# Where ScalarE's held passes stand between the projection groups of a gated mix of attention and gMLP

## The chip, the cores and the metric

The kernel runs on 1 core of a Trainium2 chip. The metric is the time of one execution on the device in microseconds (us). Each kernel has a profile of one execution; times inside it count from the start of its span.

## What is computed

One input x of 2048 tokens by 1024 goes through two branches, which a gate mixes per token:

```python
g = sigmoid((x * gate_w).sum(-1))
# A: 32 heads of 32; each token attends to itself and 7 earlier tokens, 2 apart
q, k, v = split(x @ wqkv)                  # 1024 x 3072
a = softmax(q . k[t - 2w], w = 0..7) @ v[t - 2w] @ wo
# B: gMLP, 3584 columns in two halves of 1792
z = gelu(x @ w_in); z1, z2 = z[:, :1792], layernorm(z[:, 1792:])
b = (z1 * (w_sp @ z2 + b_sp)) @ w_out      # w_sp is 2048 x 2048
out = g * a + (1 - g) * b
```

## The kernel before

TensorE computes all products; ScalarE evicts most of them from PSUM (copy or gelu); VectorE does the attention itself as elementwise products and folds; SP issues the transfers. q, k and v go through scratch in HBM and come back in another layout.

**Heads** are taken in 8 groups of 4. `qkv_tile(g, j)` (L931 on) projects one sixteenth of the tokens on a group's q, k and v: 8 matmuls of 384 columns (L936), a cast by ScalarE (L939) and, every fourth tile, three stores (L944).

**z2** has 4 column blocks of 448. The blocks 0 and 1 are plain tiles (L370, gelu L379). The blocks 2 and 3 are computed by `z2_group(u)`, u = 0 to 7, each for 256 tokens: a scheme of seven products of 4 matmuls of 449 columns (L451) in place of eight. The 449th column carries the gate's sum. Between the products stand four qkv tiles (of the groups 3 and 4 of heads), so that TensorE has work while ScalarE moves partial results. In order:

1. product a11 into bank pa; ScalarE copies pa to a second bank (the seed, L467); tile 1;
2. products s1 into bank pd and s2 onto pa; ScalarE keeps both (L445); tile 2;
3. the two late gelus of the group before (`z2_late`: L379 and a one-column L457 each); products a12 onto the seed and s3 onto pa; gelu of the seed; a third keep (L445); tile 3;
4. products s4 onto pd and a22 onto pa; two sums by VectorE (L483, and L484, which reads pd); gelu of pa; tile 4.

The product s2 writes a bank that the seed copy L467 reads, and a22 one that the third keep reads, so TensorE waits for ScalarE's queue at these two places. A tile or product that takes over pd's bank waits for L484.

**Attention** runs on VectorE beside all this, one group of heads after the other: the products q.k (L505) and their folds (L509, L512), the maximum and the difference (`soft_a`, L526 to L529), the exponentials on ScalarE (L550), sums and reciprocal (`soft_b`, L554 to L560), the products with v (L570) and their folds (L576, L577, L573). ScalarE needs another table of functions for the exponentials than for gelu; each change is a table load in its queue.

**The order of the work** is set when the program is written out, by a planner in the kernel. `Beat` counts the time of the matmuls written so far. `beat.at(t, fn)` writes a piece of work out when that clock passes t. The steps of attention carry a time at which VectorE should be free; a step is written out once that is no more than `lead` ahead of the clock: 3.0 us in general (`LEAD`), 1.0 in the groups (`GROUP_LEAD`). Engines run their queues strictly in this order.

In the groups three kinds of passes of ScalarE are **held back**. `hold_back` puts the exponentials (`exp_now`) and the absolute sum over an attention output (`o_norm_now`, L679) into the list `held`, and `release()` (L539) empties it. It is called three times in a group: behind the cast of tile 3, behind the gelu of pa, and behind the cast of tile 4. The third kind are the squares (L1011), sums of squares of one z2 tile of 1792 columns for the layer norm. Eight are owed over the groups (`prep["owed"]`: one each for u = 1 to 6, two for u = 7). They are written at the end of a group if nothing held was released in it, all that are owed at once (`squares_owed`).

**Behind the groups** come the groups 5 to 7 of heads with the rest of the z2 blocks 0 and 1, which use six banks of one pool and two of another in turn. ScalarE takes on the absolute sums over rows of w_sp (L758) there. Then come z1 (L1084, gelu L1087) and the mixing groups (L1101), seven products each again, with ScalarE's seed copies (L1125), keeps (L1111, L1113) and VectorE's sums (L1117); the column sums L799 on VectorE must be done before them.

Of the kernel before, what the change touches and what calls it, by code (L numbers as in the profile page):

```python
# [35 lines left out]
DN = ZC + 2  # L36
BEAT = 1.0 / 2360.0
LEAD = 3.0
GROUP_LEAD = 1.0
MIX_LEAD = 0.5  # L40
NU = S // 256
FL = FH // 2
# [20 lines left out]
def kernel(  # L63
# [276 lines left out]
    beat = Beat()  # L340
# [37 lines left out]
    def z2_out(src, i, c, scale):  # L378
        nc.scalar.activation(z2[:, i, ZC * c:ZC * (c + 1)], src, ACT.Gelu_apprx_tanh, scale=scale,  # L379
                             accum_out=s1[:, 4 * i + c:4 * i + c + 1])  # L380
# [61 lines left out]
    def z2_keep(ps):  # L442
        out = z2_snaps[z2_kept[0] % 5]
        z2_kept[0] += 1
        nc.scalar.copy(out, ps[:, 0:DN - 1])  # L445
        return out

    def z2_product(ps, w, v, first):
        for k in range(4):
            lhsT = w[:, k // 2, k % 2, :] if len(w.shape) == 4 else w[:, k, :]  # L450
            nc.tensor.matmul(ps[:, 0:DN - 1], lhsT, v[:, k, 0:DN - 1], start=(first and k == 0), stop=(k == 3),  # L451
                             skip_group_check=True)
        beat.run(4 * (DN - 1))

    def z2_late(i, src, scale):
        z2_out(src[:, 0:ZC], i, 3, scale)
        nc.scalar.activation(gl_s[:, i:i + 1], src[:, ZC:ZC + 1], ACT.Copy, scale=scale)  # L457
# [3 lines left out]
    def z2_group(u, tiles):  # L461
        v = tokens[u]
        scale = zinv
        pa, pd = [psum.tile([P, 512], F32, name="ps", tag="ps") for _ in range(2)]
        z2_product(pa, v.a11, m11, True)
        pb = seeded.tile([P, 512], F32, name="seed", tag="sd")
        nc.scalar.copy(pb[:, 0:DN - 1], pa[:, 0:DN - 1])  # L467
        tiles.pop(0)()
        z2_product(pd, v.s1, r1, True)
        p5 = z2_keep(pd)  # L470
        z2_product(pa, v.s2, r2, False)
        u2 = z2_keep(pa)
        tiles.pop(0)()
        while z2_wait:
            z2_late(*z2_wait.pop(0))
        z2_product(pb, v.a12, m21, False)
        z2_out(pb[:, 0:ZC], 2 * u, 2, scale)
        z2_product(pa, v.s3, r3, False)
        u3 = z2_keep(pa)
        tiles.pop(0)()  # L480
        some = release()
        z2_product(pd, v.s4, m22, False)
        TT(p5, p5, u3, ALU.add)  # L483
        TT(u2, u2, pd[:, 0:DN - 1], ALU.add)  # L484
        beat.on_vector(1.3)
        z2_product(pa, v.a22, r4, False)
        z2_out(pa[:, 0:ZC], 2 * u + 1, 2, scale)
        some = release() or some
        tiles.pop(0)()
        some = release() or some  # L490
        prep["owed"] += min(u, 1) + u // 7
        if not some:
            squares_owed(u)
        z2_wait.extend([(2 * u + 1, p5, scale), (2 * u, u2, scale)])

    L = att_L
# [34 lines left out]
    held, exp_wait = [], []  # L531
# [4 lines left out]
        else:  # L536
            fn()

    def release():  # L539
        some = bool(held)  # L540
        while held:
            held.pop(0)()
        return some

    def exp_now():
        if exp_wait:
# [185 lines left out]
    prep = {"at": 1e12, "normed": 0, "done": False, "attended": False, "heads": 0, "mixing": False, "groups": False, "owed": 0}  # L732
# [21 lines left out]
    def load_nat(a, slot):  # L754
        sync.dma_start(slot, wsp_v[a])

    def row_norm(a, slot):
        nc.scalar.activation(slot, slot, ACT.Abs, accum_out=l1[:, a:a + 1])  # L758
# [46 lines left out]
    def stats(i):  # L805
        sl = slice(i - 7, i + 1)
        s1v = s1[:, 4 * (i - 7):4 * (i + 1)].rearrange("p (i c) -> p i c", c=4)
        nc.vector.tensor_reduce(mean[:, sl], s1v, AX.X, ALU.add)
        nc.vector.tensor_scalar(mean[:, sl], mean[:, sl], 1.0 / FH, None, ALU.mult)
        nc.vector.tensor_tensor(var[:, sl], mean[:, sl], mean[:, sl], ALU.mult)  # L810
        nc.vector.scalar_tensor_tensor(var[:, sl], s2[:, sl], 1.0 / FH, var[:, sl], ALU.mult, ALU.subtract)
        nc.vector.tensor_scalar(var[:, sl], var[:, sl], 0.0, EPS, ALU.max, ALU.add)
        nc.gpsimd.tensor_tensor(rstd[:, sl], var[:, sl], cm05[:], ALU.pow)
        beat.on_vector(0.8)

    def norm(ii):
        nc.vector.tensor_scalar(z2h[:, ii, :], z2[:, ii, :], mean[:, ii:ii + 1], rstd[:, ii:ii + 1],
                                ALU.subtract, ALU.mult)
        beat.on_vector(0.75)
        prep["normed"] += 1  # L820
# [110 lines left out]
    def qkv_tile(g, j, plain=True):  # L931
        wgt = wg_slots[g % 3]
        ps = bank() if plain else psum.tile([P, 512], F32, name="ps", tag="ps")
        for kt in range(KT):
            lhsT = xT[:, kt, j * P:(j + 1) * P] if g == 0 else _sub_ap(xh_flat, kt * S + j, [[NJ, P]])
            nc.tensor.matmul(ps[:, 0:3 * C].rearrange("p (t c) -> p t c", t=3), lhsT, wgt[:, :, kt, :],  # L936
                             start=(kt == 0), stop=(kt == KT - 1))
        st = (stage_early if g < 5 else stage_slots)[stg[0] % 3]
        nc.scalar.copy(st[:, j % 4, :].rearrange("p (t d h) -> p t d h", t=3, h=HG),  # L939
                       ps[:, 0:3 * C].rearrange("p (t h d) -> p t d h", t=3, h=HG))  # L940
        if j % 4 == 3:
            row, step, first = (C, P * C, (j - 3) * P) if g == 0 else (NJ * C, C, j - 3)
            for n, (t_d, off) in enumerate(((q_d, g * S), (k_d, g * (S + 16) + 16), (v_d, g * (S + 16) + 16))):
                sync.dma_start(bass.AP(tensor=t_d.tensor, offset=t_d.offset + (off + first) * C,  # L944
                                       ap=[[row, P], [step, 4], [1, C]]), st[:, :, n * C:(n + 1) * C])
            stg[0] += 1
        projected[g] += 1
        beat.run(KT * 3 * C)
# [46 lines left out]

    square = [0]

    def squares_owed(u):
        while prep["owed"] > 0:
            prep["owed"] -= 1  # L1000
            squares(u)

    def squares(u=NU):
        i = square[0]
        square[0] += 1
        out_, src = junk[:, 0:FH], z2[:, i, :]
        if u < 4:
            out_ = wg_slots[2].rearrange("p t k c -> p (t k c)")[:, 0:FH]
        elif i < 8:
            out_, src = z2[:, 12:16, 0:ZC], src.rearrange("p (a f) -> p a f", a=4)  # L1010
        nc.scalar.activation(out_, src, ACT.Square, accum_out=s2[:, i:i + 1])  # L1011
        if i % 8 == 7:
            beat.at(beat.now + 4.0, lambda i=i: stats(i))
            for ii in range(i - 7, i + 1):
                beat.at(beat.now + 10.0, lambda ii=ii: norm(ii))
# [8 lines left out]
    tiles = [lambda g=g, j=j: qkv_tile(g, j, False) for g in (3, 4) for j in range(NJ)]  # L1024
    beat.lead = GROUP_LEAD
    prep["groups"] = True
    for u in range(NU):
        if u == 4:
            load_wg(5)
        z2_group(u, tiles)  # L1030
# [1 line left out]
        z2_late(*z2_wait.pop(0))  # L1032
    beat.lead = LEAD
    prep["groups"] = False
    release()
    squares_owed(NU)
    t = beat.now
    for n in range(16):
        beat.at(t + (0.5 + 2.5 * n if n < 3 else 5.2 * n), lambda n=n: load_nat(n, nat_slots[n % 3]))
        beat.at(t + 11.5 + 5.2 * n, lambda n=n: row_norm(n, nat_slots[n % 3]))  # L1040
    for g in range(5, NG):
# [4 lines left out]
        for j in range(NJ):  # L1046
            qkv_tile(g, j)
            n = NJ * (g - 5) + j
            if n % 3 == 2:
                n = n // 3  # L1050
# [3 lines left out]
    t = beat.now  # L1054
# [4 lines left out]
    t = beat.now  # L1059
# [133 lines left out]
    for n in range(2 * NU):  # L1193
        u, fb = n // 2, n % 2
        t = beat.now
# [21 lines left out]
    t = beat.now  # L1217
# [183 lines left out]
```

## Time and profile before

| | |
|---|---|
| time, median of 3 runs | 676.68 us (675.35 to 677.0) |
| profiled execution | 676.31 us |
| its span | 674.5 us |
| granted clock of TensorE | 1.0 |
| busy: TensorE, VectorE, ScalarE, GpSimd | 663.6, 575.7, 442.4, 12.0 us |

| stretch, us | what | TensorE busy | VectorE busy | ScalarE busy | DMA share |
|---|---|---|---|---|---|
| 92.5 to 184.2 | projection groups | 85.94 of 91.7 | 85.97 | 69.09 | 0.38 |
| 184.2 to 270 | heads 5 to 7, rest of z2 | 85.80 of 85.8 | 83.39 | 76.57 | 0.89 |
| 270 to 368 | z1 | 98.00 of 98 | 96.21 | 74.80 | 0.78 |
| 368 to 533 | mixing | 164.82 of 165 | 150.57 | 116.82 | 0.73 |

How to read it: the span is the part of an execution that the profiler records. In lists of waits a line gives engine and line, what it waited for, the total, the number of times and the longest. In a timeline a line gives start, duration, engine, line, operation and, in brackets, the idle time ahead of it and what ended it. "PE" is TensorE, "DVE" VectorE, "ACT" ScalarE. Matmuls overlap: the next starts before the one ahead has ended, so starts tell more than ends. In a table of stretches each engine has its busy time and its number of instructions, then come the granted clock, the DMA share and GB/s.

### The profile page before, as it was taken

To read this page: it belongs to the slowest core of one execution; us is meant where nothing else is said; L and a number is where in the kernel's file an instruction comes from. 1 tells how busy PE (TensorE), PEld (TensorE's weight loads), DVE (VectorE), ACT (ScalarE), POOL (GpSimd) and SP (SyncE) were. 2 spreads that over 40 slices of the span, in tenths; PEclk is the share of its full clock that TensorE was granted. 3 is DMA by queue.
4 is the path that set the end of the run, shared out by engine and by line. 5 is a ranking of instruction groups with operands and counts; after the bars stand their busy time and mean duration, and the time that the engine had idled before them with its cause. 6 is when DMAs were issued, how large, how long until landed. Compare 5 with 4: busy or idle time off the path is not lost.

```text
span 674.5 us, 9601 instructions
## 1 busy us (share of the span) xinstructions
PE 663.6 (98%) x3564; PEld 390.0 (58%) x3564; DVE 575.7 (85%) x660; ACT 442.4 (66%) x774; POOL 12.0 (2%) x68
## 2 busy tenths in 40 slices
PE   9999999989999999999999999999999999999998
PEld 4568876656677777555555555555555544444443
DVE  4567999998899999999999999999988787954745
ACT  4437676778879899898764568686767764522122
POOL 0000000000020000001000000000000000000000
PEclk9999999999999999999999999999999999999999
DMA  8999574244188999995966686549679599486211
GB/s 233 176 245 263 107 202 131 89 102 112 48 224 217 283 274 290 253 318 162 289 219 204 163 208 178 135 138 219 157 188 295 138 235 265 88 169 144 60 62 63
DMA packets 229919, 123.92 MB, mean 184 GB/s; under 512 B 191088, under 2 KB 217456, under 8 KB 229872
## 3 DMA queue, kind: packets, MB, share of 16 engines
q1 hardware_dynamic: 229872, 123.31, 69.2%
q8 instruction: 28, 0.46, 0.3%
q14 instruction: 19, 0.16, 0.1%
HBM read 63.97 MB, written 37.82 MB: 151 GB/s over the span
## 4 chain that ended last, share of the span: by engine, by line
PE 88%; DVE 7%; ACT 2%; DMA 1%; issue 1%; SPq 0%; ACTq 0%
PE ps L1101 37%; PE ps L936 15%; PE ps L1084 11%; PE seed L1101 7%; PE ps L370 6%; PE sd L936 5%; PE sd L1084 4%; PE ps L451 2%; DVE arena L509 1%; DVE arena L505 1%; DVE arena L570 1%; PE sd L370 1%; DMA arena<-in_B_w_in_dram 1%; DMA q_d<-arena 1%; DVE arena L437 0%
## 5 line engine op out<-in xcount | busy, mean ns | idle before, releaser
L1101 PE MATMUL ps<-arena 128*128 128x448 f16 (+1 forms) x1296 | 263.5, 363 | 0.2 <-ACT seed L1125 0.2
L1101 PEld LDWEIGHTS <-arena 128*128 128x128 f16 x1519 | 148.5, 98 | 154.3 <-issue 0.7
L936 PEld LDWEIGHTS <-arena 128*128 128x128 f16 (+1 forms) x1024 | 141.5, 138 | 31.2 <-issue 1.7
L936 PE MATMUL ps<-arena 128*128 128x384 bf16 x800 | 142.5, 326 | 1.3 <-DVE arena L484 1.3
L1084 PEld LDWEIGHTS <-arena 128*128 128x128 f16 x512 | 50.0, 98 | 46.6
L509 DVE TENSOR_TENSOR arena<-arena 128x4096 bf16<-128x4096 bf16 (+1 forms) x64 | 74.0, 1157 | 1.7
L1084 PE MATMUL ps<-arena 128*128 128x448 bf16 x384 | 75.4, 352 | 0.0
L505 DVE TENSOR_TENSOR arena<-arena 128x8192 bf16<-128x8192 bf16 x16 | 70.8, 4422 | 4.9 <-DMA arena<-k_d 4.7
L570 DVE TENSOR_TENSOR arena<-arena,att_A 128x8192 bf16<-128x8192 bf16 x16 | 70.7, 4420 | 0.2
L939 ACT CAST arena<-ps 128x384 bf16<-128x384 f32 x100 | 48.2, 491 | 28.7 <-PE ps L936 28.2
L1101 PE MATMUL seed<-arena 128*128 128x448 f16 (+2 forms) x223 | 48.7, 360 | 0.0
L451 PE MATMUL ps<-arena 128*128 128x449 f16 x192 | 42.5, 353 | 4.4 <-ACT seed L467 3.4
L370 PE MATMUL ps<-arena 128*128 128x448 bf16 x216 | 45.3, 352 | 0.5 <-DMA arena<-in_B_w_in_dram 0.5
L936 PE MATMUL sd<-arena 128*128 128x384 bf16 x224 | 41.0, 326 | 0.0
L1087 ACT ACTIVATE arena<-ps,x_sc 128x448 bf16<-128x448 f32 x48 | 29.6, 638 | 17.1 <-PE ps L1084 13.6
L1325 ACT ACTIVATE arena<-ps,omr 128x512 f32<-128x512 f32 x24 | 16.5, 688 | 32.7 <-PE ps L1101 32.7
L370 PEld LDWEIGHTS <-arena 128*128 128x128 f16 (+1 forms) x256 | 25.0, 98 | 22.1 <-ACT arena L355 0.6
L576 DVE TENSOR_TENSOR arena<-arena 128x4096 bf16<-128x4096 bf16 x16 | 36.6, 2288 | 0.2
L451 PEld LDWEIGHTS <-arena 128*128 128x128 f16 x224 | 21.9, 98 | 22.7 <-issue 5.2
L1259 DVE SCALAR_TENSOR_TENSOR arena<-seed,omr,arena 128x512 bf16<-128x512 f32 x8 | 6.0, 751 | 32.7 <-PE seed L1101 32.7
L758 ACT ACTIVATE arena<-arena 128x2048 bf16<-128x2048 bf16 x16 | 31.0, 1938 | 4.2 <-DMA arena<-in_B_w_sp_dram 4.2
L883 ACT ACTIVATE arena<-arena 128x896 bf16<-128x896 bf16 x32 | 30.3, 947 | 0.5
(190 smaller groups left out, 741.7 us busy)
## 6 DMA issues: line engine op xcount, KB each, us to landing
arena<-in_B_w_sp_dram SPq DMA_DIRECT2D x16, 512.0 KB, 4.1
arena<-v_d SPq DMA_DIRECT2D x8, 960.0 KB, 6.4
z_d<-arena SPq DMA_DIRECT2D x16, 448.0 KB, 4.6
arena<-z_d SPq DMA_DIRECT2D x16, 448.0 KB, 3.7
y_d<-arena SPq DMA_DIRECT2D x16, 448.0 KB, 3.2
arena<-k_d SPq DMA_DIRECT2D x7, 960.0 KB, 6.7
arena<-in_A_wqkv_dram SPq DMA_DIRECT2D x24, 256.0 KB, 4.7
q_d<-arena SPq DMA_DIRECT2D x32, 128.0 KB, 2.4
```

Source lines behind the costliest of these rows:

```text
L370: nc.tensor.matmul(ps[:, 0:N], x[:, kt, i * P:(i + 1) * P], _sub_ap(w2, kt * W2P + ZC * c, [[1, N]]), start=(kt == 0), stop=(kt == KT - 1) ...
L451: nc.tensor.matmul(ps[:, 0:DN - 1], lhsT, v[:, k, 0:DN - 1], start=(first and k == 0), stop=(k == 3), skip_group_check=True)
L505: TT(prod.rearrange("p (w j c) -> p w j c", w=W, j=8, c=C), in0, in1, ALU.mult)
L509: return lambda: TT(pv[:, :, 0:n], pv[:, :, 0:n], pv[:, :, n:2 * n], ALU.add)
L570: TT(prod.rearrange("p (w j d h) -> p w j d h", w=W, j=8, d=DH, h=HG), in0, in1, ALU.mult)
L576: return [(4.4, mul), (2.3, lambda: TT(p3[:, 0:4, :], p3[:, 0:4, :], p3[:, 4:8, :], ALU.add)), (1.2, lambda: TT(p3[:, 0:2, :], p3[:, 0:2, ...
L758: nc.scalar.activation(slot, slot, ACT.Abs, accum_out=l1[:, a:a + 1])
L883: nc.scalar.activation(waste, g_ring[n % 4][:, r], ACT.Abs, accum_out=yl[:, k:k + 1])
L936: nc.tensor.matmul(ps[:, 0:3 * C].rearrange("p (t c) -> p t c", t=3), lhsT, wgt[:, :, kt, :], start=(kt == 0), stop=(kt == KT - 1))
L939: nc.scalar.copy(st[:, j % 4, :].rearrange("p (t d h) -> p t d h", t=3, h=HG), ps[:, 0:3 * C].rearrange("p (t h d) -> p t d h", t=3, h=HG))
L1084: nc.tensor.matmul(ps[:, 0:512 if whole and kt == 0 else ZC], xh[:, kt, i * P:(i + 1) * P], _sub_ap(w1, kt * ZC, [[1, 512 if whole and kt ...
L1101: nc.tensor.matmul(ps[:, 0:c1 - c0], w[:, k, :], v[:, k, c0:c1], start=(first and k == 0), stop=(k == K - 1), skip_group_check=True)
```

## The change

Three things change, all for the time of the projection groups.

The release of held passes: `release()` now writes out one pass at most, and with `last=True` none that is the exponentials. It is called twice a group: behind the cast of tile 3, and with `last=True` behind the cast of tile 4.

The squares: two become owed in each of the groups u = 1 to 4. One is written in the first spot if nothing held went there, and one in the second spot of odd groups if nothing was held in either. What is left after the last group (three squares, as the instruction order shows) is written 6, 15 and 24 us later by the planner's clock.

`GROUP_LEAD` goes from 1.0 to 0.3.

```diff
-GROUP_LEAD = 1.0
+GROUP_LEAD = 0.3
...
         tiles.pop(0)()
+        prep["owed"] += 2 if 0 < u < 5 else 0
         some = release()
+        if not some:
+            square_owed(u)
         z2_product(pd, v.s4, m22, False)
...
         z2_out(pa[:, 0:ZC], 2 * u + 1, 2, scale)
-        some = release() or some
         tiles.pop(0)()
-        some = release() or some
-        prep["owed"] += min(u, 1) + u // 7
-        if not some:
-            squares_owed(u)
+        if not release(True) and not some and u % 2 == 1:
+            square_owed(u)
...
-    def release():
-        some = bool(held)
-        while held:
-            held.pop(0)()
-        return some
+    def release(last=False):
+        for fn in list(held):
+            if not (last and fn is exp_now):
+                held.remove(fn)
+                fn()
+                return True
+        return False
...
-    def squares_owed(u):
-        while prep["owed"] > 0:
+    def square_owed(u):
+        if prep["owed"] > 0:
             prep["owed"] -= 1
             squares(u)
+            return True
...
-    release()
-    squares_owed(NU)
+    while release():
+        pass
     t = beat.now
+    for n in range(prep["owed"]):
+        beat.at(t + 6.0 + 9.0 * n, lambda: square_owed(NU))
```

In the instruction order TensorE's list is the same. ScalarE's differs from group 1 on: squares stand in both spots of group 1 and in the first of groups 2, 4 and 6, the exponentials in the first spots of groups 3 and 7 (before: at the end of group 2 and in the first spot of group 7), the absolute sum in the first spot of group 5 as before. On VectorE, from group 3 on, L483 and L484 change places with the attention steps around them. On SP, the first load of w_sp (L755) stands ahead of a load of v (L594) and a store of an attention output (L598), where it stood between them, and a load of q and k moves ahead of a load of weights.

## The prediction

> **What bounds the kernel now.** I read the page's busy shares first, then the waits of TensorE, then the timelines of TensorE, ScalarE and VectorE over the eight projection groups (92.5 to 184.2 us), then the stretch table.
>
> ```profile
> PE 663.6 (98%) x3564; PEld 390.0 (58%) x3564; DVE 575.7 (85%) x660; ACT 442.4 (66%) x774; POOL 12.0 (2%) x68
> ```
>
> TensorE sets the time: 674.5 us of span less 663.6 leaves 10.9 us in all. Its waits by line (total, times, longest):
>
> ```profile
> PE ps L451 <- ACT seed L467: 3.4, 2, 1.7
> PE ps L936 <- DVE arena L484: 1.3, 2, 0.8
> PE ps L451 <- ACT arena L445: 1.1, 1, 1.1
> ```
>
> All three lie in the groups: 5.8 us that can be had there. Where they stand in TensorE's timeline:
>
> ```profile
> 108.13 1.46 PE L936 MATMUL ps<-arena 128*128 128x384 bf16 x8 [0.80 <-DVE arena L484]
> ...
> 130.01 1.46 PE L936 MATMUL ps<-arena 128*128 128x384 bf16 x8 [0.52 <-DVE arena L484]
> ...
> 136.15 0.93 PE L451 MATMUL ps<-arena 128*128 128x449 f16 x4 [1.08 <-ACT arena L445]
> ...
> 142.89 0.93 PE L451 MATMUL ps<-arena 128*128 128x449 f16 x4 [1.68 <-ACT seed L467]
> ...
> 176.46 0.93 PE L451 MATMUL ps<-arena 128*128 128x449 f16 x4 [1.68 <-ACT seed L467]
> ```
>
> What stands ahead of the waits in ScalarE's queue:
>
> ```profile
> 131.99 1.28 ACT L379 ACT_TABLE_LOAD   x1
> ...
> 135.58 0.52 ACT L445 COPY arena<-ps 128x449 f32<-128x449 f32 x1
> ...
> 138.79 1.71 ACT L1011 ACTIVATE arena<-arena 128x1792 bf16<-128x1792 bf16 x1
> ...
> 140.62 1.70 ACT L1011 ACTIVATE arena<-arena 128x1792 bf16<-128x1792 bf16 x1
> ...
> 142.31 0.53 ACT L467 COPY seed<-ps 128x449 f32<-128x449 f32 x1
> ```
>
> Two squares in a row at the end of group 3 keep the seed copy L467 of group 4 back; group 6 does the same to group 7 (172.36, 174.18, copy at 175.88). In group 2 the exponentials stand at the end, so the gelu table comes back only at group 3's late gelus, and the third keep, L445, is late.
>
> A wait costs more than its flag. Groups without one take 10.59 and 10.56 us (group 5 starts at 150.63, 6 at 161.22, 7 at 171.78). Group 4 took 12.41 (from 138.22), so its 1.68 cost 1.84. Group 3 took 12.49 (from 125.73): 1.92 over, 0.68 for the flag of 0.52 and 1.24 for that of 1.08. Group 7 reached its last tile 11.11 after its start, group 6 9.27: 1.84 again.
>
> **The change, part by part.** TensorE's order and instruction count stay. VectorE's order is the same up to L560 at 135.68. I walk the new ScalarE order with the durations of the rows: square 1.69 and in sequence 1.8, cast 0.38, keep and seed copy 0.41 to 0.53, gelu from PSUM 0.62, late gelu with its L457 0.85, table load 1.30 to the next start, exponentials 0.63 to the next cast and 0.75 to the next load.
>
> *Group 1* now gets two squares, one in each spot. First square 113.09 to 114.80, gelu to 115.42, cast to 115.80, second square to 117.49, seed copy to 118.03 where it ended at 117.90: 0.1 us more for group 2. It is swallowed: group 3's second tile starts at 130.01 whatever happens, since VectorE's L484 ends just before, and VectorE up to there waits for nobody. So the waits of 0.80 and 0.52 stay; the shorter lead does not reach them.
>
> *Group 3.* The table load at 131.99 is gone. Cast 131.50 to 131.88, two late gelus to 133.58, gelu to 134.19, keep ends 134.71. The last product wants it at 134.14 + 0.77 = 134.91. The 1.24 us go; the margin is 0.2.
>
> *The exponentials* come next, behind the third tile's cast (134.60 to 134.98): load to 136.28, exponentials ready at 137.03, load back to 138.33, gelu 138.95, cast 139.33, seed copy to 139.86. TensorE runs group 4 from 136.99 (130.01 + 3 x 1.30 + 4 x 0.77), reaches the second product of its third pair at 136.99 + 0.77 + 1.30 + 0.77 = 139.83, and starts it at 139.91. A wait of 1.84 becomes 0.08.
>
> *Groups 4 to 7.* One square or one absolute sum in the first spot ends before the next seed copy is due: in group 6 square to 168.53, gelu 169.15, cast 169.53, while the product it copies ends at 169.77. The 1.84 of group 7 goes. The exponentials of group 7 delay no seed copy, as no group follows.
>
> Sum for TensorE: 1.24 + 1.84 + 1.84 - 0.08 = **4.8 us** earlier at the end of the groups (last tile at 178.1 where it was 182.89).
>
> *What is late next.* VectorE idled 1.45 before L483 at 158.97, 1.73 at 181.94, 1.26 before L554 at 184.37 and 0.42 before L811 at 191.96: 4.86 us. In the new order it never waits there: L483/L484 come when the keep is long done (149.5, 160.3, 170.5, 181.3 against keeps that end at 145.4, 156.0, 166.6, 177.2), and the statistics stand later. But it now waits for the exponentials of group 3: wanted at 134.06, ready at 137.03, 2.97 us. Net it is 4.86 - 2.97 = 1.9 us earlier, TensorE 4.8, so VectorE is 2.9 us later against TensorE. From 192 to 376 VectorE has no gap of 0.2 us to make that up:
>
> ```profile
> 270.00:368.00 98.00, 98.00 (x520) 50.59 (x518) 96.21 (x87) 74.80 (x113) 3.13 (x15) 1.00 0.78 239
> ```
>
> (96.21 of 98 us is VectorE.) So I check each place where others need it. The column sums L799 end at 356.3 and are needed at 369.6: 13 us of cover. Exponentials run on ScalarE at 267.14 and 310.08, 3.8 and 4.1 us after L529 ended: covered. The next set is not:
>
> ```profile
> 371.29 0.69 DVE L529 TENSOR_TENSOR att_L<-att_L,att_m 128x512 f32<-128x512 f32 x1
> ```
>
> ScalarE starts its table load at 373.47, 1.5 us after this ends. Being 2.9 late makes ScalarE wait 1.4 us in the first mixing group. Behind it in the queue stand the table load, a cast and the keep L1113 (375.91 to 376.54), for which TensorE's seventh product waits, due at 368.08 + 6 x 1.513 = 377.16. The slack is 0.57 with 0.05 of signalling, so TensorE loses 1.4 + 0.05 - 0.57 = **0.9 us**. Then VectorE's gaps (0.25, 0.22, 0.96, 0.29, 0.77 up to 411) take up the rest, and the last exponentials (453.14, L529 ended 450.76) have 2.4 us.
>
> *The stage behind the groups* (184 to 270) gets three squares at planned times where it had two at its head: 1.7 us more for ScalarE, busy 76.6 of 85.8 us. TensorE has eight banks there, six tiles of 1.30 and two of 1.51, 10.8 us; ScalarE's lag at its gelus is about 2 us (TensorE's tile ended 200.6, gelu 202.46). Cover is enough: 0 us; without it, 1.7. On SP's queue the first load of w_sp moves ahead of v and of the store of o. v is wanted at about 204.5, was issued at 190.68, and no v transfer took over 7.9 us, so even late it is there: 0.
>
> Unknown sizes: the 0.08 can be 0 to 0.6 (a queue of eleven passes, 0.05 each); the 0.9 can be 0 (if VectorE gains 2 us more) to 2.8 (if it gains nothing: 4.8 - 1.5 + 0.05 - 0.57). I take the walked values.
>
> The profiled execution took 676.31 us, 1.8 around its span of 674.5, and lies 0.4 under the median of 676.68. 676.31 - 4.8 + 0.9 = **672.4 us**.
>
> [...] Each switch of table set shows 1.28 us with 0.02 us of idle ahead (cast ends 184.33, load 184.35). [...]
>
> **The rivals.**
> *All of the gain stays.* VectorE is less late than walked, and the first mixing group does not wait: 676.31 - 4.8 = 671.5.
> *VectorE gives more back.* It gains nothing in the groups and the first mixing group loses 2.8: 674.3. For it: 96% busy. Against: four gaps that have a named end.
> [...]
> *It does not do what it says.* The passes move, and new waits of the same size stand behind the first spots: 676.3. Against: every first spot has 1.1 us or more before the next seed copy, save groups 1 and 3.
> *Slower.* In the stage behind, ScalarE's queue stops at L758 until the first w_sp load lands (before: 2.82 us, at 199.82). ScalarE would come there at about 191.8. If the load landed at 199.8 again, the lag of 8 is under 10.8 and costs nothing; it decides from 202.6 on, us for us, and passes the 3.9 us of gain at 206.5. At 209, with 1.7 more for the third square, 680.5. Against: the load now stands ahead of v in SP's queue and would be issued at about 185.7 (cast of the last group tile to 181.8, its stores 1.6, three weight loads 2.2), where it was 191.94.
>
> **How the numbers follow.** Forecast 0.55, all kept 0.17, more given back 0.13, double switch 0.04, no effect 0.05, slower 0.06. The range, 670.8 to 675.0, goes from all kept less 0.7 of spread between runs (675.35 to 677.0) to the two giving-back cases plus 0.7; it leaves out some 0.15. 0.3%, 2 us, is what a measurement of this kernel tells from no change. The cases at 674.1 and 674.3 lie on that bound and are halved. Faster 0.55 + 0.17 + 0.08 = 0.80, same 0.05 + 0.09 = 0.14, slower 0.06.
>
> **What would show it.** Right: no wait of TensorE on L445, under 0.3 us on L467, the 0.80 and 0.52 still there, the last group tile near 178.1; VectorE idle about 3 us before the first L554 of the groups; a wait of about 0.9 in the first mixing group, behind an exponential that waited for L529. Wrong: a seed copy still late in group 4 or 7, a second idle stretch of VectorE in the groups, TensorE waiting between 184 and 270, or no gain left at 390.

## The result and the profile after

| | before | after |
|---|---|---|
| time, median | 676.57 us (6 runs, 675.35 to 677.0) | 672.43 us (6 runs, 671.37 to 673.44) |
| ratio to before, 95% interval | | 0.9939 [0.9926, 0.9953] |
| profiled execution, its span | 676.31, 674.5 us | 671.37, 669.6 us |

The changed kernel is 4.1 us faster; 672.4 had been forecast. Its page says first that TensorE has nearly no idle time left: 669.6 of span less 663.5 of work is 6.1 us, where it was 10.9.

```profile
PE 663.5 (99%) x3564; PEld 389.8 (58%) x3564; DVE 575.2 (86%) x660; ACT 441.6 (66%) x774; POOL 9.4 (1%) x68
```

TensorE's waits by line (total, times, longest), the longest outside the kernel's start. The edits shift the line numbers: L484 is now L487, L936 is L938, and the mixing's product L1101 and keep L1113 are L1106 and L1118:

```profile
PE ps L938 <- DVE arena L487: 0.7, 2, 0.5
PE ps L1106 <- ACT arena L1118: 0.6, 1, 0.6
```

All waits of L451 have gone; one on a keep in the mixing is new. The same in TensorE's timeline (start, duration, in brackets the idle time ahead and what ended it):

```profile
107.25 1.46 PE L938 MATMUL ps<-arena 128*128 128x384 bf16 x8 [0.20 <-DVE arena L487]
...
129.12 1.46 PE L938 MATMUL ps<-arena 128*128 128x384 bf16 x8 [0.47 <-DVE arena L487]
...
177.25 2.76 PE L938 MATMUL ps<-arena 128*128 128x384 bf16 x16
...
372.25 6.21 PE L1106 MATMUL ps<-arena 128*128 128x448 f16 x32 [0.57 <-ACT arena L1118]
```

The first two lines are the second tiles of groups 1 and 3, for which VectorE is late as before. The third line is the last tile of the groups. It comes 48.13 us after the second tile of group 3; before, 52.88 (130.01 to 182.89): **4.75 us** are gone there. The fourth is the first mixing group, where some of it is lost again.

ScalarE at the end of group 3 and the start of group 4 has the exponentials between two table loads, and the seed copy right behind the cast:

```profile
134.20 1.28 ACT L552 ACT_TABLE_LOAD   x1
135.50 0.73 ACT L552 ACTIVATE att_L<-att_L,x_sc 128x512 f32<-128x512 f32 x1
136.24 1.28 ACT L379 ACT_TABLE_LOAD   x1
137.54 0.63 ACT L379 ACTIVATE arena<-ps,yl 128x448 bf16<-128x448 f32 x1
...
138.52 0.55 ACT L467 COPY seed<-ps 128x449 f32<-128x449 f32 x1
```

VectorE waits for those exponentials, its only idle time of 0.2 us or more from group 3 to 406 us:

```profile
136.26 0.43 DVE L556 TENSOR_TENSOR att_m<-att_L 128x256 f32<-128x256 f32 x1 [3.00 <-ACT att_L L552]
```

In the first mixing group ScalarE waits for VectorE in turn, and the keep for which TensorE waits at 372.25 stands behind that wait:

```profile
369.13 1.28 ACT L552 ACT_TABLE_LOAD   x1 [1.32 <-DVE att_L L529]
...
371.57 0.62 ACT L1118 ACTIVATE arena<-ps,bt 128x448 f32<-128x448 f32 x1
```

The chain of what ended last shows the change of roles. Before, TensorE had 88% of it and VectorE 7%; now:

```profile
PE 55%; DVE 40%; ACT 3%; issue 2%; DVEq 0%; ACTq 0%
```

**What one profile can tell.** The two spans differ by 4.9 us, and 0.9 of it lies ahead of the change: the second tile of group 3 starts at 129.12 where it started at 130.01. That tile waits for VectorE, whose order up to there is the same. So below, traces are compared from the start of this tile to the end of the span: 544.49 us before, 540.48 after. The change is worth **4.0 us** there. Spans are given to 0.1 us, so differences of such figures under 0.1 say nothing. Medians of all runs stand beside it.

### The profile page after: what moved, and what is told of

Read it like the earlier page. It is cut to its first block, busy times and chain, and to the rows that moved or that the text cites. A ratio compares the mean times of both kernels' runs of the same rounds, so it can differ in the third digit from the quotient of the medians.

```text
span 669.6 us, 9598 instructions
## 1 busy us (share of the span) xinstructions
PE 663.5 (99%) x3564; PEld 389.8 (58%) x3564; DVE 575.2 (86%) x660; ACT 441.6 (66%) x774; POOL 9.4 (1%) x68
## 4 chain that ended last, share of the span: by engine, by line
PE 55%; DVE 40%; ACT 3%; issue 2%; DVEq 0%; ACTq 0%
PE ps L1106 36%; DVE arena L509 8%; DVE arena L505 7%; DVE arena L572 7%; PE seed L1106 6%; PE ps L938 6%; DVE arena L578 3%; PE ps L370 2%; DVE arena L801 2%; PE sd L938 2%; DVE arena L579 2%; DVE arena L819 2%; DVE arena L575 1%; DVE att_L L512 1%; PE sd L370 1%
## 5 line engine op out<-in xcount | busy, mean ns | idle before, releaser
L1106 PE MATMUL ps<-arena 128*128 128x448 f16 (+1 forms) x1296 | 263.7, 363 | 0.7 <-ACT arena L1118 0.6
L1106 PEld LDWEIGHTS <-arena 128*128 128x128 f16 x1519 | 148.5, 98 | 155.0 <-issue 1.5
L938 PEld LDWEIGHTS <-arena 128*128 128x128 f16 (+1 forms) x1024 | 141.4, 138 | 30.6 <-issue 1.1
L938 PE MATMUL ps<-arena 128*128 128x384 bf16 x800 | 142.5, 326 | 0.7 <-DVE arena L487 0.7
L505 DVE TENSOR_TENSOR arena<-arena 128x8192 bf16<-128x8192 bf16 x16 | 70.8, 4422 | 4.4 <-DMA arena<-k_d 4.1
L572 DVE TENSOR_TENSOR arena<-arena,att_A 128x8192 bf16<-128x8192 bf16 x16 | 70.7, 4420 | 0.2
L1106 PE MATMUL seed<-arena 128*128 128x448 f16 (+2 forms) x223 | 48.7, 360 | 0.0
L451 PE MATMUL ps<-arena 128*128 128x449 f16 x192 | 42.3, 353 | 0.0
L938 PE MATMUL sd<-arena 128*128 128x384 bf16 x224 | 41.0, 326 | 0.0
L578 DVE TENSOR_TENSOR arena<-arena 128x4096 bf16<-128x4096 bf16 x16 | 36.6, 2287 | 0.2
L451 PEld LDWEIGHTS <-arena 128*128 128x128 f16 x224 | 21.9, 98 | 18.1 <-issue 0.5
```

Source lines behind the costliest of these rows:

```text
L505: TT(prod.rearrange("p (w j c) -> p w j c", w=W, j=8, c=C), in0, in1, ALU.mult)
L572: TT(prod.rearrange("p (w j d h) -> p w j d h", w=W, j=8, d=DH, h=HG), in0, in1, ALU.mult)
L578: return [(4.4, mul), (2.3, lambda: TT(p3[:, 0:4, :], p3[:, 0:4, :], p3[:, 4:8, :], ALU.add)), (1.2, lambda: TT(p3[:, 0:2, :], p3[:, 0:2, ...
L1106: nc.tensor.matmul(ps[:, 0:c1 - c0], w[:, k, :], v[:, k, c0:c1], start=(first and k == 0), stop=(k == K - 1), skip_group_check=True)
```

## The experiments

Each of the twelve kernels was timed beside runs of the kernel before on the same chip. "From group 3" is the stretch just named, from each kernel's own trace.

### The parts alone

**The lead alone**, in the kernel before:

```diff
-GROUP_LEAD = 1.0
+GROUP_LEAD = 0.3
```

> The kernel before with only the shorter lead (GROUP_LEAD 0.3). It leaves TensorE's order as it is, changes ScalarE's order only behind the groups, and moves VectorE's L483/L484 behind the attention steps around them. Theory (the stalls belong to ScalarE's queue): TensorE keeps its waits of 1.68, 1.68 and 1.08 us, and the time stays at 676.6, within 0.3 us. Rival (the shorter lead brings part of the gain because VectorE's sums free the banks earlier): the waits of 0.80 and 0.52 on L484 shrink and the time falls by 0.5 to 1.3 us.

Measured: 676.4 us beside 676.73, ratio 0.9992 [0.9982, 1.0002]; from group 3 544.55. TensorE's waits in the groups are those of before:

```profile
PE ps L451 <- ACT seed L467: 3.4, 2, 1.7
PE ps L936 <- DVE arena L484: 1.3, 2, 0.7
...
PE ps L451 <- ACT arena L445: 1.1, 1, 1.1
```

By itself the lead brings nothing that can be measured.

**The spots alone**: the changed kernel with the old lead.

```diff
-GROUP_LEAD = 0.3
+GROUP_LEAD = 1.0
```

> The changed kernel with the lead back at 1.0, so that only the spots differ from the kernel before. The step that consumes the exponentials is then given out early enough to write them itself: in group 3 they stand ahead of the third keep L445, no longer behind the cast of tile 3. Theory: table load and exponentials (1.30 + 0.63 us) push the keep from an end at 133.8 to 135.75 in the changed kernel's trace; the last product wants it at 134.0, so TensorE waits 1.8 us there, the 0.08 at the seed copy of group 4 goes, VectorE gets its exponentials 0.9 us earlier and is no longer late in the first mixing group, which saves the 0.7 us lost there: 672.4 + 1.8 - 0.1 - 0.7 = 673.4 us. Rival (the lead does nothing for ScalarE, as the prediction put it: the shorter lead does not reach the waits): 672.4.

Measured: 673.2 us, ratio 0.9953 [0.9937, 0.9969]; from group 3 541.50, 1.0 more than the changed kernel, as the theory had it; the intervals of the two ratios overlap, so the traces decide here. TensorE has one wait more, and ScalarE's order in group 3 shows why:

```profile
136.38 0.93 PE L451 MATMUL ps<-arena 128*128 128x449 f16 x4 [1.72 <-ACT arena L445]
```

```profile
133.89 1.28 ACT L552 ACT_TABLE_LOAD   x1
135.19 0.72 ACT L552 ACTIVATE att_L<-att_L,x_sc 128x512 f32<-128x512 f32 x1
135.82 0.52 ACT L445 COPY arena<-ps 128x449 f32<-128x449 f32 x1
```

Load and exponentials stand ahead of the keep L445. The step that sums them (`soft_b`) writes them itself if they have not been released by then; with the lead of 1.0 it is given out before the first spot of group 3. So the shorter lead is worth about 1 us, but only together with the spots.

**The squares alone**: exponentials may go into the second spot again, and a second square only into group 1.

```diff
-        if not release(True) and not some and u % 2 == 1:
+        if not release() and not some and u == 1:
```

> The changed kernel with one edit: the exponentials may also go into the second spot, and a second square only into group 1. So the exponentials stand at the end of group 2 as in the kernel before, and the squares stand one at a time. Theory: the two waits behind double squares go (2 x 1.84 us), the 1.24 us of group 3 stays (gelu's table comes back only ahead of the late gelus there), VectorE does not wait for exponentials and is not late afterwards, so nothing is given back in the mixing: 676.6 - 3.7 = 672.9 us, with one wait of about 1.1 us on L445 in group 3. Rival (the gain stems from moving the exponentials): 675 or more.

Measured: 672.99 us beside 676.73, ratio 0.9945 [0.9927, 0.9962]. The stall of group 3 is there, those behind double squares are not; 0.3 us at the seed copy of group 3 are new, since it stands behind square and exponentials (the tile behind it has no flagged wait for VectorE here, so they are not all extra):

```profile
PE ps L451 <- ACT arena L445: 1.1, 1, 1.1
...
PE ps L451 <- ACT seed L467: 0.3, 1, 0.3
```

So most of the gain comes from writing the squares one at a time. The interval of this kernel overlaps that of the changed kernel: the times alone do not tell the two apart.

**The exponentials alone**: the old rule for the squares.

```diff
-        prep["owed"] += 2 if 0 < u < 5 else 0
         some = release()
-        if not some:
-            square_owed(u)
...
-        if not release(True) and not some and u % 2 == 1:
-            square_owed(u)
+        prep["owed"] += min(u, 1) + u // 7
+        if not release(True) and not some:
+            while square_owed(u):
+                pass
```

> The changed kernel with the old rule for the squares (all that are owed at the end of a group in which nothing was held); the exponentials stand in the first spot of group 3 as in the changed kernel. The double squares then stand at the ends of groups 4 and 6. Theory: group 3 loses its 1.24 us of stall and group 4 its 1.84 (0.08 stays), group 5 gets a new one of 1.84 behind the double square, group 7 keeps its 1.84; VectorE's 3.0 us of wait for the exponentials are taken from idle time it has anyway: 676.6 - 1.24 - 1.84 + 0.08 + 1.84 = 675.4 us. Rival (the double squares cost nothing and the table is the whole cause): 672 to 673.

Measured: 675.42 us, ratio 0.9983 [0.9974, 0.9992]; from group 3 543.44, 1.05 less than before. The double squares now end groups 4 and 6, and their stalls have moved to groups 5 and 7 with them:

```profile
151.96 0.93 PE L451 MATMUL ps<-arena 128*128 128x449 f16 x4 [1.68 <-ACT seed L467]
...
174.94 0.93 PE L451 MATMUL ps<-arena 128*128 128x449 f16 x4 [1.68 <-ACT seed L467]
```

### What a square in the second spot costs

**A second square in group 6**:

```diff
-        if not release(True) and not some and u % 2 == 1:
+        if not release(True) and not some and (u % 2 == 1 or u == 6):
```

> The changed kernel with a square in the second spot of group 6 too, so that group 7's seed copy again stands behind a square. Theory: TensorE loses 1.84 us in group 7; since VectorE is then 1.84 us less late against TensorE, the 0.7 us of the first mixing group come back: 672.4 + 1.84 - 0.7 = 673.5 us. Rival A (the loss counts whole): 674.3. Rival B (a second square fits): 672.4.

Measured: 675.0 us, ratio 0.9977 [0.9967, 0.9986]; from group 3 542.19, 1.7 more than the changed kernel. But the theory falls: TensorE has no wait in group 7 that the list shows. The loss is at the keep in the first mixing group, 2.16 us where it was 0.57, since VectorE has a second wait, for GpSimd's `rstd`:

```profile
374.95 5.27 PE L1106 MATMUL ps<-arena 128*128 128x448 f16 x27 [2.16 <-ACT arena L1118]
```

```profile
213.61 5.34 DVE L819 TENSOR_SCALAR arena<-arena,mean,rstd 128x1792 f16<-128x1792 bf16 x8 [1.55 <-POOL rstd L815]
```

The added square also changed how many are left for behind the groups: two, not three. The eighth square of a half sets the time of the statistics (L810 to L815, 4 us later by the planner's clock) and of the normalisation L819 that needs them (10 us later). With one square fewer left, only one sum (L578, 2.28 us) stands between the two in VectorE's queue; in the changed kernel six attention steps do, from 212.37 to 218.96. To tell the two effects apart, **the square of group 4 was taken out**, so that three are left:

```diff
-        if not some:
+        if not some and u != 4:
             square_owed(u)
...
-        if not release(True) and not some and u % 2 == 1:
+        if not release(True) and not some and (u % 2 == 1 or u == 6):
```

> The changed kernel with a square in both spots of group 6 and none in group 4, so that three squares are left for behind the groups, as in the changed kernel, and not two as in the version that only added a square to group 6. That version's trace shows 0.1 us of loss at the seed copy of group 7, and a new wait of VectorE, 1.55 us for GpSimd's rstd (L815), since the statistics come one square earlier. Theory: that wait is what it lost, through the keep L1118 in the first mixing group; with three left the wait is gone: 672.5 us. Rival (the second square in group 6 itself is what costs): 674 to 675.

Measured: 673.02 us, ratio 0.9937 [0.9925, 0.9949]; from group 3 540.55, the changed kernel's figure within rounding. The wait for `rstd` is gone. Two squares in a group cost next to nothing if each has a spot of its own; what cost 1.84 us in the kernel before was two in a row at the group's end.

### Where the rest went

**More work for VectorE**: the first sum over the exponentials of one group of heads four times, with the same result. The edit takes the third group of heads (`g == 2`). Its exponentials stand in the first spot of projection group 7; those for which VectorE waits at 136 us belong to the group of heads before.

```diff
-        TT(att_m[:], L4[:, :, 0:4, :], L4[:, :, 4:8, :], ALU.add)
+        for _ in range(4 if g == 2 else 1):
+            TT(att_m[:], L4[:, :, 0:4, :], L4[:, :, 4:8, :], ALU.add)
```

> The changed kernel with three more passes of VectorE: the first sum of soft_b for the exponentials of group 3 is done four times (0.43 us each, 1.3 us in all, the result is the same). Theory (behind the 3.0 us of wait VectorE has no slack left up to the first mixing group): the 1.3 us are paid whole, part of them in TensorE's waits for L487 in groups 5 to 7, the rest in the first mixing group: 673.7 us. Rival (VectorE's time is hidden, TensorE alone sets the time): 672.4.

Measured: 674.24 us, ratio 0.9965 [0.9951, 0.9978]; from group 3 541.93, 1.45 more than the changed kernel for 1.3 us of work. It is paid whole, all at the keep of the first mixing group (here L1119), 1.9 us where it was 0.57.

```profile
PE ps L1107 <- ACT arena L1119: 1.9, 1, 1.9
```

The four passes take 1.80 us where the one took 0.42:

```profile
183.80 1.80 DVE L557 TENSOR_TENSOR att_m<-att_L 128x256 f32<-128x256 f32 x4
```

They come behind the last group (its last tile starts at 179.20 here), so the part that the theory put into the waits for L487 in groups 5 to 7 could not arise. The run shows that VectorE has nothing to spare from 184 us to the first mixing group; for 137 to 184 us the missing idle time is all there is to show it.

**The exponentials of the mixing behind that keep**:

```diff
-    held, exp_wait = [], []
+    held, exp_wait, behind_keep = [], [], []
...
-            beat.at(t + 1.0, lambda: hold_back(exp_now))
+            beat.at(t + 1.0, lambda: behind_keep.append(exp_now) if prep["mixing"] else hold_back(exp_now))
...
         u3 = keep(pa, hi)
+        while behind_keep:
+            behind_keep.pop(0)()
```

> The changed kernel, but in the mixing the exponentials are written behind the keep of the third partial product (L1118), so that this keep does not stand behind ScalarE's wait for VectorE. VectorE needs those exponentials some 17 us later. Theory: the wait of 0.57 us on L1118 goes, and with it the 0.7 us given back: 671.7 us. Rival (the late VectorE takes the time at another place of the mixing): 672.4.

Measured: 672.48 us, ratio 0.9936 [0.9924, 0.9947]. The wait on L1118 is gone, and from group 3 it takes 539.74 us, 0.7 less than the changed kernel, as expected. The ratios do not separate the two kernels: 0.7 us is within the interval of either.

**Gelu's table in ScalarE's idle time**: the exponentials at the end of group 2, one gelu of one column (result not used) behind the second keep of group 3.

```diff
         u2 = z2_keep(pa)
+        if u == 3:
+            nc.scalar.activation(wsc[:, 3:4], cm05[:, 0:1], ACT.Gelu_apprx_tanh)
...
-        if not release(True) and not some and u % 2 == 1:
+        if not release() and not some and u == 1:
```

> The exponentials stand at the end of group 2 again, the squares one at a time, and one gelu of a single column (its result is not used) stands in group 3 behind the second keep, where ScalarE had 1.39 us of idle time. It brings gelu's table back there, not ahead of the late gelus. Theory: all three stalls of the groups go (1.24 + 1.84 + 1.84 us), VectorE does not wait 3.0 us for the exponentials, so it is not late in the first mixing group and nothing is given back there: 676.6 - 4.9 = 671.7 us, 0.7 under the changed kernel. Rival (the wait for the exponentials in group 3 is not what makes the mixing group late, or VectorE finds other waits): 672.4.

Measured: 672.27 us, ratio 0.9929 [0.9917, 0.9941]. In this kernel the second tile of group 3 does not wait for VectorE, so its trace is counted from the second tile of group 1: 561.80 us to the end, where the changed kernel has 562.35. Here too two squares are left and VectorE waits 1.55 us for `rstd`; and TensorE waits 0.30 and 0.17 us in group 3. With **no square in group 2**, three are left:

```diff
-        if not some:
+        if not some and u != 2:
             square_owed(u)
```

> The version with the exponentials at the end of group 2 and gelu's table brought back in ScalarE's idle time, now with no square in group 2, so that three are left. Theory: the 0.30 us at the seed copy of group 3 and the 0.17 at its keep go (no square ahead of the exponentials in group 2), the 1.55 us of VectorE's wait for GpSimd go, but TensorE then waits for L487 again in group 3 (0.47): 671.7 us, 0.7 under the changed kernel. Rival (nothing left to gain there): 672.4.

Measured: 672.11 us, ratio 0.9923 [0.9910, 0.9936]; from group 1 561.62, 0.7 less than the changed kernel. VectorE's wait for `rstd` is gone; at the seed copy of group 3 TensorE still waits 0.20 us, where the theory had nothing. The table load lies in ScalarE's gap:

```profile
131.04 1.28 ACT L474 ACT_TABLE_LOAD   x1
132.34 0.20 ACT L474 ACTIVATE wsc<-cm 128x1 f32<-128x1 f32 x1
```

**The changed kernel again**, beside the last three:

> The changed kernel itself, unaltered, beside the three variants on the same chip: 672.4 us, within 0.5.

Measured: 672.89 us beside 677.28, ratio 0.9947 [0.9931, 0.9963]; from group 3 540.46 and from group 1 562.33, as in its first trace. So the version above is 0.8 us faster than it on the same chip (672.11 to 672.89). Against the kernel before it is clearly faster; its interval overlaps that of the changed kernel, so that it beats this one too rests on the traces more than on the times.

**A lead of -1.5 in group 2, with the exponentials of the mixing behind the keep** (that edit stands above; only the lead is shown):

```diff
     for u in range(NU):
+        beat.lead = {2: -1.5}.get(u, GROUP_LEAD)
```

> The changed kernel with the exponentials of the mixing behind the keep L1118, and in group 2 alone a lead of -1.5 in place of 0.3: the sums L486/L487 then stand ahead of the product L572 (4.42 us) there, for which TensorE waited 0.47 us at the second tile of group 3. Theory: 0.7 us of the mixing group and 0.5 us of group 3 go: 672.4 - 1.2 = 671.2 us. Rival (VectorE pays elsewhere for standing still ahead of the sums, as it has no slack): 671.7 or more.

Measured: 679.18 us, ratio 1.0032 [1.0020, 1.0044], slower than before; from group 1 it takes 568.0 us. What the theory named did happen: the waits on L1118 and at the second tile of group 3 are gone. But VectorE's attention steps slip in the mixing. Up to 430 us the passes L505, L572 and L575 start within 1.6 us of where they stand in the changed kernel's second trace; from 438 us on some are late, and the last L575 ends at 510.6 us where it was 498.5. The sums over the heads that follow are late, and TensorE waits for them:

```profile
PE ps L1107 <- DVE arena L716: 4.1, 2, 2.6
```

Against the 561.1 that the theory comes to from group 1, the lead of one group thus cost some 7 us, in a stage 400 us later: 4.1 us are the waits, and a granted clock of 0.50 behind them costs, by an estimate at the end of this text, 2.6 more. Which step of the planner carried it there was not followed further.

## Why the prediction was right, point by point

- **The total**: 672.4 against 672.43 is closer than the method is good for. The walk started from an execution of 676.31 us, where the median of all runs before is 676.57, and it had 3.9 us of gain where the medians give 4.1. That these two differences cancel is luck; the terms below are not.
- **The stalls of the groups** (1.24 + 1.84 + 1.84 - 0.08 = 4.8): measured 4.75 over the same stretch. The 0.08 left at the seed copy of group 4 was about 0.2: its two products take 1.73 us up to the next tile (138.15 to 139.88), where others take 1.53. It is too short for the list of waits. The traces of the parts place them: 1.08 of flag (the idle time in brackets) on L445 stays with the squares alone, 1.68 comes twice behind double squares with the exponentials alone.
- **Waits that stay**: 0.52 was 0.47. The 0.80 was 0.20, but it varies from run to run ahead of the change: 1.12 in the second trace of the same kernel. It was no part of the gain.
- **VectorE's wait for the exponentials**: 2.97 forecast, 3.00 measured, and no idle time after it until the mixing.
- **ScalarE's wait in the first mixing group**: 1.4 forecast, 1.32 measured. TensorE's loss there was put at 0.9. The flag is 0.57; with the exponentials moved behind the keep 0.7 us come back. The term was 0.2 too large. Part of that is a slip in the sum: from 376.54 to 377.16 are 0.62 us, and 0.57 is what is left when the 0.05 of signalling is taken off (before, the keep L445 ends at 136.10 and its product starts at 136.15); the sum then adds the 0.05 once more. With 0.62 and the measured 1.32 it is 1.32 + 0.05 - 0.62 = 0.75.
- **The stage behind the groups** at no cost: TensorE was busy in 86.00 of 86.00 us from 184 to 270 us in the changed kernel's second trace. That VectorE loses nothing there held only because three squares are left; with two, 1.55 us are lost. The prediction did not see that this hung on the number.
- **The rival by the table switch**: the 0.04 for a double switch and the case at 674.1 would need a load that holds ScalarE for twice its row, and no run shows one. In the changed kernel load, exponentials, load and gelu start 1.30, 0.74 and 1.30 us apart (134.20 to 137.54), and the loads take 1.28. What ends at 184.33 in the trace before, 0.02 us ahead of a load, is the exponentials (183.60, 0.73 us), not a cast.
- **The other rivals**: that nothing is given back would have been 4.8; it was 4.0. That the end is on the other side, through ScalarE waiting for w_sp, did not come: no wait of that kind reaches TensorE.
- **What the prediction left out**: what the shorter lead is for. "The shorter lead does not reach them" is right for the waits on L484, and the lead alone changes nothing. But in the new order it keeps `soft_b` from writing the exponentials ahead of the third keep of group 3, which would cost 1.0 us. The walk had this order from the instruction list, so the sum did not suffer; the reason for it was missing.

Of the 4.1 us, then, the squares written one at a time bring about 3.7 (the squares-alone kernel, which pays 0.3 at a seed copy); the exponentials moved out of group 2's end bring the stall of 1.24 and give back 0.2 at the seed copy of group 4 and 0.7 through VectorE.

## What to carry to other kernels

What ScalarE did on the side cost here by its place in the queue and not by its sum: two squares of 1.7 us were free with one in each of two gaps (540.55 us from group 3 beside 540.46), where two in one gap cost 1.84 us, the second pass whole. When the bounding engine speeds up, walk the next engine's slack forward to the place where it is first needed; here that place was 230 us further on, and the price could be read from three rows. A parameter of a planner reaches as far as its clock does, so compare the written order of every engine to the end of the kernel.

## What the runs showed of the hardware

**The clock after a stall.** In the last version TensorE waited 2.59 us for L716, up to 536.43, and 1.50 us, up to 539.82. Busy time and granted clock by stretch (the columns are length, then TensorE, weight loads, VectorE, ScalarE and GpSimd busy, the granted clock, DMA share and GB/s):

```profile
532.00:536.00 4.00, 1.84 (x10) 0.76 (x8) 3.13 (x10) 2.56 (x6) 0.00 (x0) 1.00 0.93 192
536.00:540.00 4.00, 2.07 (x5) 0.56 (x6) 3.90 (x8) 0.57 (x1) 0.00 (x0) 0.53 1.11 251
540.00:544.00 4.00, 4.00 (x12) 1.42 (x11) 3.90 (x10) 1.23 (x2) 0.00 (x0) 0.62 1.11 250
544.00:548.00 4.00, 4.00 (x20) 1.86 (x19) 2.93 (x6) 3.56 (x8) 0.00 (x0) 1.00 0.98 198
```

From 537 to 543 us the granted clock is 0.50: 12 matmuls from 540 to 544 where the next 4 us have 20. An estimate from these rows: TensorE worked for some 5.1 us at half the clock (2.07 up to 540, 3 up to 543), and half of that, 2.6 us, is lost. With the waits that makes 6.7 of the 7 us.

By single microseconds the clock is 1.00 from 535 to 536 us, 0.62 from 536 to 537 and 0.97 from 543 to 544. So it goes down about where the wait of 2.59 us ends (536.43), before the second wait begins (538.32). In the kernel before it is 1.00 through and behind both waits of 1.68 us (141 to 147 and 174 to 180 us). That the wait of 2.59 us brought it down is inferred from this order alone; no run varied the length of a wait, and why the clock fell is not shown.

**GpSimd beside VectorE.** The same `rstd` step of 128x8 took 3.62 us in the version with a second square in group 6 and 2.01 us in the changed kernel:

```profile
209.96 3.62 POOL L815 TENSOR_TENSOR rstd<-var,cm 128x8 f32<-128x8 f32 x1 [5.22 <-DVE var L814]
```

```profile
212.55 2.01 POOL L815 TENSOR_TENSOR rstd<-var,cm 128x8 f32<-128x8 f32 x1 [8.81 <-DVE var L814]
```

In the first, VectorE ran a sum of 128x4096 (L578, 209.78, 2.28 us) at the same time, in the second one of 128x1024 (0.68 us). The last version has a case between, beside a sum of 128x2048 (L579, 212.13, 1.22 us):

```profile
212.31 2.55 POOL L815 TENSOR_TENSOR rstd<-var,cm 128x8 f32<-128x8 f32 x1 [7.55 <-DVE var L814]
```

In all three GpSimd's step ends 1.5 us after VectorE's sum has ended (212.06 to 213.58, 213.05 to 214.56, 213.35 to 214.86), so it took the longer, the longer the sum beside it. VectorE shows no delay in turn: in the changed kernel its passes L526 to L529 start inside the 2.01 us of `rstd` 0.46, 0.32 and 0.26 us apart, where the kernel before has them 0.45, 0.32 and 0.27 apart at 122.82. No run here varied the sum alone, so why the step takes longer is not shown.
